# A layer norm ahead of the first matmuls, split over VectorE and ScalarE in a fixed order with dummy matmuls between

## The chip, the cores and the metric

The kernel runs on one core of a Trainium2 chip. The time is device time in microseconds (us) of one execution. Every set of runs was measured beside runs of the kernel before on the same chip, in alternating rounds. The core has one TensorE (PE, matmuls), one VectorE (DVE), one ScalarE (ACT), and a SyncE (SP) that issues most of the DMA transfers.

## The reference, cut to what matters

```python
x = A_x                                                # 2048 tokens x 1024
x = x + attention(layernorm(x), wqkv, wo)              # 32 heads of 32; each token sees 8 keys, 2 apart
x = x + swiglu(layernorm(x), w1, w3, w2)               # 1024 -> 3584 -> 1024
x = x + attention(layernorm(x), wqkv, wo)              # the same two layers again
x = x + swiglu(layernorm(x), w1, w3, w2)
```

The attention needs no large matmul for its scores. It is products and sums on VectorE. Projections and MLP are dense bf16 matmuls on TensorE. The first layer norm stands alone in front of everything: until its first chunk (512 tokens, four tiles of 128) is normalised and transposed, no real matmul can start. I call this stretch the prefix.

## The kernel before

TensorE's order is fixed by hand (`manual_schedule`). The order on VectorE, ScalarE and SyncE is decided by a scheduler, which works with priorities and with its own estimate of when things are ready.

```python
    x_sb = const.tile([P, S // P, D], BF16, name="x_sb")
    for j in range(TPC):                                   # TPC = 4 tiles in a chunk
        nc.sync.dma_start(x_sb[:, j:j + 1, :], xin[:, j:j + 1, :])
    ...
    for i in range(NWARM):                                 # 16 dummy matmuls, for the clock
        pw = bank("pw")
        nc.tensor.matmul(pw[:], lhsT=hT[:, 0, 0:P], rhs=hT[:, 0, :], start=True, stop=True)
    ...
        def stats(j):                                      # in ln_first, the prefix
            for hh in range(2):
                nc.vector.bn_stats(st[:, hh, :], x_sb[:, j, hh * 512:(hh + 1) * 512])
            nc.vector.bn_aggr(mv[:], st[:])
            nc.scalar.activation(sd[:], mv[:, 1:2], ACTF.Sqrt, bias=epst[:])
        def apply(j, mv, sd):
            nc.vector.reciprocal(rstd[:], sd[:])
            nc.vector.tensor_scalar(xn[:], x_sb[:, j, :], mv[:, 0:1], rstd[:], op0=ALU.subtract, op1=ALU.mult)
            for kk in range(KT):
                nc.tensor.transpose(pT[:, kk, :], xn[:, kk * P:(kk + 1) * P], ident[:])
            nc.scalar.copy(xnT[:, :, j * P:(j + 1) * P], pT[:])
    ...
    # q_part: "ps" matmuls of q, k or v of one chunk, copied out of PSUM by ScalarE, stored to DRAM
                nc.scalar.copy(sgt[:, t - t0, :], ps[:])   # sgt has 3 buffers
            nc.sync.dma_start(qkv_d[l][which][:, t0:t0 + SG, c * CH:(c + 1) * CH], sgt[:])
    # t_scores: loads qT and kT back, then on VectorE per window step w_
            nc.vector.tensor_tensor(pr[:], qT[:], kT[:, :, k0:k0 + TCH], op=ALU.mult)
            tree_sum8(pr, psm[:, w_, :])
    ...     # then transpose, sums, maximum, and on ScalarE
        nc.scalar.activation(E[:], L[:], ACTF.Exp, scale=scale)
    # b_stage: MLP; VectorE makes one hT tile per pair of matmul groups
                        nc.scalar.activation(sg[:], pg[:], ACTF.Silu)
                        nc.vector.tensor_tensor(hT[:, g0 + fi - f0, :], sg[:], pu[:], op=ALU.mult)
    # loads through SyncE's queue in program order: x chunks, wo (2 MB), w1t and w3t (1 MB each), kT, vT ...
```

## Time and profile before

The time before was 1636.41 us in the median of 3 runs (1635.89 to 1637.51). The span of the profiled run is 1635.4 us.

| what | value | view |
|---|---|---|
| TensorE / VectorE / ScalarE busy | 99% / 70% / 21% | page, part 1 |
| first real matmul (ps) | 13.92 us | timeline |
| first attention product (pr) | 56.59 us | timeline of VectorE |
| VectorE full | from 57 to about 530 us | slices of the page |
| TensorE's waits after the prefix | 0.66 + 4.86 + 2.11 + 1.86 + 0.75 = 10.2 us, the last at 425 us | timeline of TensorE |

From the page of the kernel before, the span, parts 1 and 2 (the digits are tenths of busy time in 40 slices of 41 us):

```profile
span 1635.4 us, 18944 instructions
...
PE 1616.1 (99%) x7472; PEld 800.2 (49%) x7472; DVE 1152.4 (70%) x1961; ACT 340.5 (21%) x530; POOL 1.9 (0%) x12
...
DVE  4899999999999781897728977299652992332212
```

TensorE is 99% busy, so a shorter prefix can give at most the time that TensorE loses there. VectorE is the second limit: it is full in slices 3 to 13. While it is full, TensorE waits for it now and then.

The timeline of the kernel before in the prefix (columns: start us, busy us, engine, line, operation, out<-in, form, count, and in brackets the idle time before it with its releaser):

```profile
3.81 1.29 DVE L149 BATCH_NORM_STATS2 st_165<-x_sb 128x6 f32<-128x512 bf16 x2 [2.53 <-DMA x_sb<-in_A_x_dram]
...
11.60 0.55 DVE L159 TENSOR_SCALAR xn<-x_sb,mv_215,rstd_235 128x1024 bf16<-128x1024 bf16 x1
12.20 0.62 PE L162 MATMUL pT<-ident,xn 128*128 128x128 bf16 x8 [0.96 <-DVE xn L159]
12.86 1.01 ACT L163 COPY xnT<-pT 128x1024 bf16<-128x1024 bf16 x1 [0.57 <-PE pT L162]
13.92 2.29 PE L202 MATMUL ps<-xnT,wqkv 128*128 128x512 bf16 x5 [1.10 <-ACT xnT L163]
```

The last tile is the bottleneck of the prefix: normalise, transpose, copy of 1.01 us, first matmul. The five matmuls in that last line take 2.29 us, 0.46 each, about twice what they take later (the whole stretch of 640 takes 139.71 us, 0.22 each). The clock shows why. The same kernel in stretches (from:to and length, then busy time and count by engine, granted TensorE clock, DMA share, GB/s):

```profile
13.50:17.00 3.50, 3.08 (x8) 1.27 (x8) 1.84 (x4) 0.37 (x1) 0.00 (x0) 0.53 1.05 387
195.00:210.00 15.00, 10.14 (x40) 4.24 (x39) 14.05 (x23) 7.66 (x12) 0.00 (x0) 0.89 0.89 254
```

The granted clock was 0.53 behind the first ps matmul: nearly the whole stretch at half speed. The clock record of the trace gives half speed from 13.40 to 16.81 us on the time axis of these views, 3.41 us (the prediction below means the same window, read 0.09 us late). Near 200 us, behind TensorE's longest wait, there is one more such window.

VectorE's timeline of the kernel before, at the start of attention:

```profile
56.59 2.36 DVE L228 TENSOR_TENSOR pr<-qT,kT 128x2048 bf16<-128x2048 bf16 x2 [3.38 <-DMA kT<-qkv_d_1_159]
...
86.08 0.43 DVE L247 TENSOR_TENSOR e_537<-E 128x256 f32<-128x256 bf16 x1 [0.70 <-ACT E L245]
```

The first product waited 3.38 us for kT. The issues on SyncE's queue of the kernel before, just ahead of that:

```profile
45.27 0.37 SPq L205 DMA_DIRECT2D qkv_d_1_159<-sgt  x1
45.69 0.46 SPq L356 DMA_DIRECT2D wo<-in_A_wo_dram  x1
48.87 0.53 SPq L213 DMA_DIRECT2D kT<-qkv_d_1_159  x1
...
53.91 0.47 SPq L297 DMA_DIRECT2D w1t<-in_B_w_dram  x1
```

kT can be issued when the last K store (45.27) has landed. Here wo goes behind that store and w1t behind kT.

TensorE's timeline of the kernel before, its waits after the prefix (between them it runs without a gap that matters):

```profile
187.09 8.85 PE L202 MATMUL ps<-xnT,wqkv 128*128 128x512 bf16 x40 [0.66 <-DVE x_sb L287]
200.80 3.28 PE L305 MATMUL pg<-xnT,w1t 128*128 128x512 bf16 x8 [4.86 <-DMA xnT<-xn]
263.25 24.56 PE L327 MATMUL acc<-w2t,hT 128*128 128x512 bf16 x113 [2.11 <-DVE hT L314]
347.30 18.52 PE L327 MATMUL acc<-w2t,hT 128*128 128x512 bf16 x85 [1.86 <-DVE hT L314]
425.06 24.56 PE L327 MATMUL acc<-w2t,hT 128*128 128x512 bf16 x113 [0.75 <-DVE hT L314]
```

At 507 us TensorE needs the 56th hT tile, the last of the second MLP unit (28 tiles each). In this profile that tile is finished at 507.26 us, just when it is needed, so no wait shows.

### The profile page before, as it was taken

How to read it: one execution, taken by the hardware profiler on the slowest of the kernel's cores; microseconds unless marked ns; L12 is line 12 of the kernel's file. 1: busy time of each engine (PE TensorE's matmuls, PEld its weight loads, DVE VectorE, ACT ScalarE, POOL GpSimd, SP SyncE). 2: the span in 40 equal slices, each digit the busy share in tenths (PEclk: the TensorE clock that was granted, in tenths of full speed). 3: DMA queues.
4: the chain of work that ended last, by engine and by line, in shares of the span. 5: the costliest groups of instructions: out<-in, count | busy, mean ns of one | idle time of the engine just before them, and what ended most of it. 6: DMA issues, size and time to landing. Idle time of an engine off the chain costs nothing.

```text
span 1635.4 us, 18944 instructions
## 1 busy us (share of the span) xinstructions
PE 1616.1 (99%) x7472; PEld 800.2 (49%) x7472; DVE 1152.4 (70%) x1961; ACT 340.5 (21%) x530; POOL 1.9 (0%) x12
## 2 busy tenths in 40 slices
PE   8999899999999999999999999999999999999999
PEld 5666444444444644446444554445544444444444
DVE  4899999999999781897728977299652992332212
ACT  3333311203021320223202232022320211121110
POOL 0000000000000000000000000000000000000000
PEclk9999999999999999999999999999999999999999
DMA  9943746557546774367743686438753574256440
GB/s 297 280 132 102 220 158 195 159 151 209 183 131 180 240 235 150 106 193 245 221 142 104 199 259 200 142 104 249 255 178 119 129 232 155 90 143 205 155 129 26
DMA packets 337113, 286.32 MB, mean 175 GB/s; under 512 B 69632, under 2 KB 319488, under 8 KB 336896
## 3 DMA queue, kind: packets, MB, share of 16 engines
q1 hardware_dynamic: 337024, 285.11, 57.2%
q8 instruction: 58, 0.95, 0.2%
q14 instruction: 31, 0.25, 0.0%
HBM read 239.99 MB, written 29.36 MB: 165 GB/s over the span
## 4 chain that ended last, share of the span: by engine, by line
PE 67%; DVE 29%; issue 3%; DMA 1%; ACT 0%; DVEq 0%; ACTq 0%
PE acc L327 21%; PE pg L305 15%; PE pu L309 15%; PE ps L202 13%; DVE pr L228 5%; DVE tm L273 4%; PE po L283 3%; DVE hT L314 3%; DVE tm L174 3%; DVE pr L174 2%; DVE x_sb L287 1%; DVE st L124 1%; DVE tm L175 1%; DVE pr L175 1%; DVE L L235 1%
## 5 line engine op out<-in xcount | busy, mean ns | idle before, releaser
L305 PE MATMUL pg<-xnT,w1t 128*128 128x512 bf16 x1792 | 424.7, 380 | 4.9 <-DMA xnT<-xn 4.9
L309 PE MATMUL pu<-xnT,w3t 128*128 128x512 bf16 x1792 | 423.7, 379 | 0.0
L327 PE MATMUL acc<-w2t,hT 128*128 128x512 bf16 x1792 | 390.8, 379 | 5.1 <-DVE hT L314 4.7
L202 PE MATMUL ps<-xnT,wqkv 128*128 128x512 bf16 x1536 | 334.3, 380 | 1.8 <-ACT xnT L163 1.1
L313 ACT ACTIVATE sg<-pg 128x512 bf16<-128x512 f32 x224 | 133.4, 597 | 843.2 <-PE pg L305 831.4
L314 DVE TENSOR_TENSOR hT<-sg,pu 128x512 bf16<-128x512 bf16 x224 | 152.1, 679 | 212.2 <-PE pu L309 210.7
L305 PEld LDWEIGHTS <-w1t 128*128 128x128 bf16 x1792 | 175.5, 98 | 217.0 <-issue 6.6
L327 PEld LDWEIGHTS <-hT 128*128 128x128 bf16 x1792 | 174.8, 98 | 218.5 <-DVE hT L314 9.0
L309 PEld LDWEIGHTS <-w3t 128*128 128x128 bf16 x1792 | 175.5, 98 | 212.0 <-issue 1.0
L202 PEld LDWEIGHTS <-wqkv 128*128 128x128 bf16 x1536 | 220.5, 144 | 114.6 <-issue 3.9
L332 DVE TENSOR_TENSOR x_sb<-x_sb,acc 128x512 bf16<-128x512 bf16 x128 | 87.0, 680 | 162.2 <-PE acc L327 162.2
L228 DVE TENSOR_TENSOR pr<-qT,kT 128x2048 bf16<-128x2048 bf16 x128 | 153.1, 1210 | 51.6 <-issue 32.1
L273 DVE TENSOR_TENSOR tm<-At,vT 128x2048 bf16<-128x2048 bf16 x128 | 151.7, 1213 | 0.3
L204 ACT CAST sgt<-ps 128x512 bf16<-128x512 f32 x192 | 108.7, 588 | 184.6 <-PE ps L202 151.7
L283 PE MATMUL po<-wo,oT 128*128 128x512 bf16 x512 | 115.4, 379 | 0.0
L124 DVE BATCH_NORM_STATS2 st<-x_sb 128x6 f32<-128x512 bf16 x120 | 79.9, 681 | 18.0 <-DMA x_sb<-in_A_x_dram 17.3
L174 DVE TENSOR_TENSOR pr<-pr 128x1024 bf16<-128x1024 bf16 x128 | 85.6, 680 | 0.0
L174 DVE TENSOR_TENSOR tm<-tm 128x1024 bf16<-128x1024 bf16 x128 | 84.4, 681 | 0.0
L283 PEld LDWEIGHTS <-oT 128*128 128x128 bf16 x512 | 50.0, 98 | 60.4
L287 DVE TENSOR_TENSOR x_sb<-x_sb,po 128x512 bf16<-128x512 bf16 x64 | 43.2, 677 | 15.4 <-PE po L283 15.4
L175 DVE TENSOR_TENSOR pr<-pr 128x512 bf16<-128x512 bf16 x128 | 51.8, 415 | 0.2
L175 DVE TENSOR_TENSOR tm<-tm 128x512 bf16<-128x512 bf16 x128 | 50.3, 415 | 0.1
(169 smaller groups left out, 428.7 us busy)
## 6 DMA issues: line engine op xcount, KB each, us to landing
w1t<-in_B_w_dram SPq DMA_DIRECT2D x56, 1024.0 KB, 5.4
w3t<-in_B_w_dram SPq DMA_DIRECT2D x56, 1024.0 KB, 7.2
w2t<-in_B_w_dram SPq DMA_DIRECT2D x48, 1024.0 KB, 5.4
wqkv<-in_A_wqkv_dram SPq DMA_DIRECT2D x28, 1024.0 KB, 6.6
w2t<-in_B_w_dram SPq DMA_DIRECT2D x16, 512.0 KB, 5.1
qkv_d_0_158<-sgt SPq DMA_DIRECT2D x16, 256.0 KB, 5.3
qkv_d_1_159<-sgt SPq DMA_DIRECT2D x16, 256.0 KB, 4.4
qT<-qkv_d_0_158 SPq DMA_DIRECT2D x8, 512.0 KB, 4.0
```

The costliest lines, as they stand in the source:

```text
L174: nc.vector.tensor_tensor(buf[:, 0:4, :], buf[:, 0:4, :], buf[:, 4:8, :], op=ALU.add)
L175: nc.vector.tensor_tensor(buf[:, 0:2, :], buf[:, 0:2, :], buf[:, 2:4, :], op=ALU.add)
L202: nc.tensor.matmul(ps[:], lhsT=ws[kk // KH][:, kk % KH, t::KT], rhs=xnT[:, kk, :], start=(kk == 0), stop=(kk == KT - 1))
L204: nc.scalar.copy(sgt[:, t - t0, :], ps[:])
L228: nc.vector.tensor_tensor(pr[:], qT[:], kT[:, :, k0:k0 + TCH], op=ALU.mult)
L273: nc.vector.tensor_tensor(tm[:], At[:], win, op=ALU.mult)
L283: nc.tensor.matmul(ps[:], lhsT=oT[:, t, j * P:(j + 1) * P], rhs=wo[:, t, hh * 512:(hh + 1) * 512], start=(t == 0), stop=(t == KT - 1))
L305: nc.tensor.matmul(pg[:], lhsT=w1t[:, kk, fi * P:(fi + 1) * P], rhs=xnT[:, kk, :], start=(kk == 0), stop=(kk == KT - 1))
L309: nc.tensor.matmul(pu[:], lhsT=w3t[:, kk, fi * P:(fi + 1) * P], rhs=xnT[:, kk, :], start=(kk == 0), stop=(kk == KT - 1))
L313: nc.scalar.activation(sg[:], pg[:], ACTF.Silu)
L314: nc.vector.tensor_tensor(hT[:, g0 + fi - f0, :], sg[:], pu[:], op=ALU.mult)
L327: nc.tensor.matmul(acc[:], lhsT=hT[:, f - f0, j * P:(j + 1) * P], rhs=w2ts[(f - f0) // 8][:, (f - f0) % 8, :], start=(f == f0), stop=(f == ...
```

## The change

The intent: make the prefix shorter and keep TensorE's clock up. The last tile's statistics go to ScalarE (a sum in one pass, a sum of squared deviations in a second). The order on VectorE and ScalarE is fixed by hand. The PSUM copies of the last two tiles are made in halves, one by each engine. Ten of the dummy matmuls stand between the transposes; 13 instead of 16 stand in front. Two of the four first loads are issued from ScalarE's queue.

```diff
-    NWARM = 16
+    NWARM = 13
 ...
-        nc.sync.dma_start(x_sb[:, j:j + 1, :], xin[:, j:j + 1, :])
+        (nc.scalar if j % 2 else nc.sync).dma_start(x_sb[:, j:j + 1, :], xin[:, j:j + 1, :])
 ...
+        def apply(j):
 ... (cut: as before; the last tile uses ScalarE's sums, (x + (-mean)) * rstd)
+            kn = KT if j < 2 else KT // 2
 ... (cut: transposes into KT // kn PSUM tiles)
+        def evacuate(j, pTs):
+            kn = KT // len(pTs)
+            for h, pT in enumerate(pTs):
+                copy = nc.vector.tensor_copy if h else nc.scalar.copy
+                copy(xnT[:, h * kn:(h + 1) * kn, j * P:(j + 1) * P], pT[:])
+
+        warm(NWARM)
+        with hp(), tc.manual_schedule(engines={mybir.EngineType.PE, mybir.EngineType.DVE,
+                                               mybir.EngineType.Activation}):
+            stats(0, 0)
+            stats(0, 1)
+            deviation(0)
+            stats(1, 0)
+            nc.scalar.activation(junk[:], x_sb[:, last, :], ACTF.Copy, accum_out=am[:, 0:1])
+            nc.scalar.mul(am[:, 1:2], am[:, 0:1], -1.0 / D)
+            pT0 = apply(0)
+            warm(4)
+            stats(1, 1)
+            deviation(1)
+            nc.scalar.activation(junk[:], x_sb[:, last, :], ACTF.Square, bias=am[:, 1:2], accum_out=am[:, 2:3])
+            stats(2, 0)
+            pT1 = apply(1)
+            warm(4)
+            evacuate(0, pT0)
+            deviation(last)
+            stats(2, 1)
+            deviation(2)
+            evacuate(1, pT1)
+            pT2 = apply(2)
+            warm(2)
+            pT3 = apply(3)
+            evacuate(2, pT2)
+            evacuate(3, pT3)
```

The diff ends in the prefix, but its effect does not. With different emission the scheduler also puts what follows in another order on VectorE, ScalarE and SyncE. In SyncE's queue wo moves ahead of the last K store, and w1t ahead of kT. On VectorE, hT and x_sb updates of the first two MLP units come 1 to 4 us of work earlier. In the traces VectorE has the same instructions ahead of the 56th hT tile in both orders, but for one short reciprocal, in another sequence; the sequences of VectorE and ScalarE become the same at about 531 us.

More of the change, by code (lines that the diff above doesn't have):

```diff
@@ L101, with warm @@
     nc.scalar.activation(preload[:], epst[:], ACTF.Sqrt)
-    for i in range(NWARM):
-        pw = bank("pw")
-        nc.tensor.matmul(pw[:], lhsT=hT[:, 0, 0:P], rhs=hT[:, 0, :], start=True, stop=True)
+    def warm(n):
+        for i in range(n):
+            pw = bank("pw")
+            nc.tensor.matmul(pw[:], lhsT=hT[:, 0, 0:P], rhs=hT[:, 0, :], start=True, stop=True)
     wo = const.tile([P, KT, D], BF16, name="wo")
@@ L143, in ln_first @@
         xnT = xnTs[key] = xtp.tile([P, KT, CH], BF16, name="xnT")
-        def stats(j):
-            st = small.tile([P, 2, 6], FP32, name="st1")
-            mv = small.tile([P, 2], FP32, name="mv1", bufs=2)
-            for hh in range(2):
-                nc.vector.bn_stats(st[:, hh, :], x_sb[:, j, hh * 512:(hh + 1) * 512])
-            nc.vector.bn_aggr(mv[:], st[:])
-            sd = small.tile([P, 1], FP32, name="sd1", bufs=2)
-            nc.scalar.activation(sd[:], mv[:, 1:2], ACTF.Sqrt, bias=epst[:])
-            return mv, sd
@@ L155, in apply @@
-        def apply(j, mv, sd):
-            rstd = small.tile([P, 1], FP32, name="rstd1")
-            nc.vector.reciprocal(rstd[:], sd[:])
-            xn = xnp.tile([P, D], BF16, name="xn")
-            nc.vector.tensor_scalar(xn[:], x_sb[:, j, :], mv[:, 0:1], rstd[:], op0=ALU.subtract, op1=ALU.mult)
-            pT = psum.tile([P, KT, P], BF16, name="pT", tag="mm")
-            for kk in range(KT):
-                nc.tensor.transpose(pT[:, kk, :], xn[:, kk * P:(kk + 1) * P], ident[:])
-            nc.scalar.copy(xnT[:, :, j * P:(j + 1) * P], pT[:])
@@ L165, in ln_first @@
-        with hp():
-            held = stats(0)
-            for j in range(1, TPC):
-                nxt = stats(j)
-                apply(j - 1, *held)
-                held = nxt
-            apply(TPC - 1, *held)
+        last = TPC - 1
+        st = small.tile([P, last, 2, 6], FP32, name="st1", bufs=1)
+        mv = small.tile([P, last, 2], FP32, name="mv1", bufs=1)
+        sd = small.tile([P, TPC], FP32, name="sd1", bufs=1)
+        rstd = small.tile([P, TPC], FP32, name="rstd1", bufs=1)
@@ new lines, in ln_first, with stats, deviation @@
+        am = small.tile([P, 3], FP32, name="am", bufs=1)
+        junk = xnp.tile([P, D], BF16, name="xn")
+        def stats(j, hh):
+            nc.vector.bn_stats(st[:, j, hh, :], x_sb[:, j, hh * 512:(hh + 1) * 512])
+        def deviation(j):
+            if j < last:
+                nc.vector.bn_aggr(mv[:, j, :], st[:, j, :, :])
+                nc.scalar.activation(sd[:, j:j + 1], mv[:, j, 1:2], ACTF.Sqrt, bias=epst[:])
+            else:
+                nc.scalar.activation(sd[:, j:j + 1], am[:, 2:3], ACTF.Sqrt, bias=epst[:], scale=1.0 / D)
@@ new lines, in apply @@
+        def apply(j):
+            nc.vector.reciprocal(rstd[:, j:j + 1], sd[:, j:j + 1])
+            xn = xnp.tile([P, D], BF16, name="xn")
+            if j < last:
+                nc.vector.tensor_scalar(xn[:], x_sb[:, j, :], mv[:, j, 0:1], rstd[:, j:j + 1],
+                                        op0=ALU.subtract, op1=ALU.mult)
+            else:
+                nc.vector.tensor_scalar(xn[:], x_sb[:, j, :], am[:, 1:2], rstd[:, j:j + 1],
+                                        op0=ALU.add, op1=ALU.mult)
+            kn = KT if j < 2 else KT // 2
+            pTs = []
+            for k0 in range(0, KT, kn):
+                pT = psum.tile([P, kn, P], BF16, name="pT", tag="mm")
+                for kk in range(k0, k0 + kn):
+                    nc.tensor.transpose(pT[:, kk - k0, :], xn[:, kk * P:(kk + 1) * P], ident[:])
+                pTs.append(pT)
+            return pTs
```

## The prediction

> **What bounds the kernel now.** The page: TensorE 99% busy, VectorE 70%. The timeline: real matmuls start at 13.92 us and run dense until 187 us. TensorE's waits up to 425 us are 0.66 (for x_sb), 4.86 (xnT at 200.8), 2.11, 1.86, 0.75 us (hT): 10.2 us., then none. The chain of waits runs through VectorE and DMA from 57 to 260 us, and the slices show VectorE full from 57 to about 530 us. So between 57 and 507 us the attention work on VectorE sets the pace, and TensorE has slack before it.
>
> **What the change does to the prefix.** Now: statistics from 3.81, last normalisation 11.60, last transposes 12.20, last PSUM copy 12.86 to 13.88 (1.01 us on ScalarE). The clock record shows TensorE at half speed from 13.49 to 16.90 (3.41 us): some 7 matmuls at 0.425 instead of 0.216 us, 1.5 us lost. The Trainium skill (TensorE: Matmul & The Clock Gate, Part 1) describes such an activity window of about 3.4 us; this trace agrees. The added 10 dummies should keep the clock up.
> Removed from VectorE: two statistics (2 x 0.6) and one aggregation. Added: two half copies out of PSUM, estimated 0.4 to 0.6 us each. ScalarE gets two passes over 1024 elements, estimated 1.0 us each from its 1.01 us copy, plus one small operation. Its work from 5.3 us on sums to 6.7 us and gaps. I expect ScalarE to be the prefix's limit and the first real matmul at 12.5 to 13.5 us. Issuing two loads from ScalarE saves only issue time (0.4 us each).
> TensorE should then be 2 to 2.5 us ahead at 20 us.
>
> **Why little of it should reach the end.** Attention starts at 56.59 us, when kT lands. The stores before it wait for ScalarE, which waits (2.2 us at 44.3) for statistics of x tiles whose load lands at 39.1; the DMA engines are nearly full from 28 to 60 us. This timing follows DMA, not TensorE. The instruction order also changes: wo's 2 MB load now precedes the last K store, and w1t's 1 MB load precedes kT. At 350 to 390 GB/s (estimate) kT lands 0 to 3 us later. In return the new VectorE order puts hT and x_sb updates of the first two MLP stages 1 to 4 us of work earlier, so the waits at 263 to 425 us shrink; but hT number 56 (507 us, which now finishes just in time) has the same VectorE work before it in both orders. So the end moves by what attention's start moves, about -2 to +3 us.
>
> **Prediction.** 1636.5 us, range 1632.8 to 1639.8. Faster by over 2%: 0.5%; within 2%: 99%; slower by over 2%: 0.5%.
>
> **What would show it.** Right: the first ps matmul near 13 us at full clock; the first pr later than 55.5 us; larger TensorE waits at 187/200 or 507 us, smaller ones at 263 and 347 us. Wrong on the prefix: half clock still behind the first ps matmul, or a start later than 13.9. Wrong on the absorption: pr starts 2 us earlier and the whole time falls by over 3 us.
>
> **What would make it wrong.** kT not delayed by the loads ahead of it; the reordered VectorE work shifting hT number 56; accumulating ScalarE passes costing much more than a copy; the clock window's phase, which decides also whether half clock returns after the wait at 200 us (about 1.7 us).

## The result, and the profile after

The changed kernel took 1637.5 us in the median of 6 runs (1635.92 to 1638.35), the kernel before 1636.84 us in the same rounds (6 runs, 1635.89 to 1637.71). Ratios here and below are those for the runs of the same rounds. They lie within 0.0002 of the ratio of the mean times, and are not quite the ratio of the quoted medians. The ratio is 1.0003 with a 95% interval of 0.999 to 1.0016: the same. The profiled run happens to be the fastest of the six. A second profile of the same kernel (e5 below, span 1636.3 us) has the same three waits, 5.52, 2.49 and 2.92 us.

From the page after, the span and part 1:

```profile
span 1633.9 us, 18952 instructions
...
PE 1616.6 (99%) x7479; PEld 800.8 (49%) x7479; DVE 1151.9 (70%) x1960; ACT 341.9 (21%) x534; POOL 1.9 (0%) x12
```

The timeline of the prefix after:

```profile
4.92 1.29 DVE L157 BATCH_NORM_STATS2 st_133<-x_sb 128x6 f32<-128x512 bf16 x2 [3.64 <-DMA x_sb<-in_A_x_dram]
...
6.69 1.04 ACT L197 ACTIVATE xn<-x_sb 128x1024 bf16<-128x1024 bf16 x1
...
7.63 0.19 ACT L197 ACTIVATION_READ_ACCUMULATOR xn<-x_sb 128x1 f32 x1
...
8.73 1.13 ACT L203 ACTIVATE xn<-x_sb,am 128x1024 bf16<-128x1024 bf16 x1
...
12.19 0.55 DVE L173 TENSOR_SCALAR xn<-x_sb,am,rstd_136 128x1024 bf16<-128x1024 bf16 x1
...
13.38 0.59 ACT L188 COPY xnT<-pT 128x512 bf16<-128x512 bf16 x1 [0.29 <-PE pT L180]
13.60 0.42 DVE L188 COPY xnT<-pT 128x512 bf16<-128x512 bf16 x1 [0.45 <-PE pT L180]
14.02 2.32 PE L247 MATMUL ps<-xnT,wqkv 128*128 128x512 bf16 x10 [0.45 <-ACT xnT L188]
```

The work itself became shorter: from the first statistics to the first ps matmul it is 14.02 - 4.92 = 9.10 us, before 13.92 - 3.81 = 10.11 us. But it starts 1.11 us later, because the first tile lands later, so the first matmul is not earlier. What did change is the pace: ten matmuls in 2.32 us, not five in 2.29 us. The half copies, 0.59 us on ScalarE and 0.42 us on VectorE, replace the one of 1.01 us. The stretches after:

```profile
13.50:17.00 3.50, 3.05 (x16) 2.01 (x14) 3.15 (x7) 1.05 (x2) 0.00 (x0) 1.00 1.05 390
195.00:210.00 15.00, 11.31 (x40) 4.59 (x41) 14.03 (x21) 5.55 (x10) 0.00 (x0) 0.77 0.80 228
```

The clock stays full behind the first matmul (1.00 for 0.53). Near 200 us it is worse in this run, two windows at half speed for one. The first copy of a finished ps tile starts at 15.94 us for 17.26 us before, so TensorE is 1.3 us ahead there.

VectorE's timeline after, at the start of attention:

```profile
57.29 2.36 DVE L273 TENSOR_TENSOR pr<-qT,kT 128x2048 bf16<-128x2048 bf16 x2 [7.82 <-DMA kT<-qkv_d_1_127]
```

The issues on SyncE's queue after, ahead of that:

```profile
40.22 0.91 SPq L401 DMA_DIRECT2D wo<-in_A_wo_dram  x1
43.15 0.36 SPq L250 DMA_DIRECT2D qkv_d_1_127<-sgt  x1
...
46.32 0.46 SPq L342 DMA_DIRECT2D w1t<-in_B_w_dram  x1
52.19 0.52 SPq L258 DMA_DIRECT2D kT<-qkv_d_1_127  x1
```

The last K store is issued 2.1 us earlier than before, and VectorE is ready far earlier (it waits 7.82 us, not 3.38). But kT is issued 9.0 us after that store instead of 3.6 us, now that wo is in the queue ahead of the store and w1t ahead of kT. So attention starts 0.7 us later than before, not earlier.

TensorE's waits after the prefix:

```profile
198.69 3.57 PE L350 MATMUL pg<-xnT,w1t 128*128 128x512 bf16 x8 [4.94 <-DMA xnT<-xn]
343.72 18.52 PE L372 MATMUL acc<-w2t,hT 128*128 128x512 bf16 x85 [1.59 <-DVE hT L359]
505.85 18.52 PE L372 MATMUL acc<-w2t,hT 128*128 128x512 bf16 x85 [2.91 <-DVE hT L359]
```

The waits at 187, 263 and 425 us are gone. Those of 2.11 and 0.75 us (2.86 together) were for hT, and a new wait for hT of 2.91 us has come at 506 us, at the 56th tile. TensorE arrives there earlier and waits for VectorE instead. The sum is 9.4 us, before 10.2 us.

### The profile page after: what moved, and what is told of

Read it like the earlier page. It is cut to its first block, busy times and chain, and to the rows that moved or that the text cites. A ratio compares the mean times of both kernels' runs of the same rounds, so it can differ in the third digit from the quotient of the medians.

```text
span 1633.9 us, 18952 instructions
## 1 busy us (share of the span) xinstructions
PE 1616.6 (99%) x7479; PEld 800.8 (49%) x7479; DVE 1151.9 (70%) x1960; ACT 341.9 (21%) x534; POOL 1.9 (0%) x12
## 4 chain that ended last, share of the span: by engine, by line
PE 68%; DVE 27%; issue 2%; DMA 2%; ACT 1%; SPq 0%; DVEq 0%
PE acc L372 21%; PE pg L350 17%; PE pu L354 16%; PE ps L247 10%; DVE pr L273 5%; DVE tm L318 4%; PE po L328 3%; DVE hT L359 2%; DVE tm L219 2%; DVE pr L219 2%; DVE st L127 2%; DVE x_sb L332 1%; DVE pr L220 1%; DVE tm L220 1%; DVE oT L221 1%
```

## The experiments

Two theories stood against each other at the start.

- A, "absorbed": what the prefix gains is lost on the way, because attention's start and its VectorE work set the end. What the changed order of later instructions does is a second, separate effect.
- B, "nothing gained": the prefix itself gains nothing (the first matmul is no earlier), the dummies are idle ornament, and the order does not matter.

To separate prefix and order I pinned the order of everything after the prefix on SyncE, VectorE and ScalarE, by a list, with dependencies that order instructions without any semaphore. Pinning the changed kernel to its own order gave the identical instruction order on every engine. All experiments but e5 carry this addition:

```diff
+PINNED = {"SP": [...], "DVE": [...], "ACT": [...]}     # emission numbers, in the wanted order
 ...
+    names = {i.name: i for i in nc.cur_bb.bb.instructions}
+    for todo in PINNED.values():
+        for first, then in zip(todo, todo[1:]):
+            tc.add_manual_dep(names[f"I-{BASE[0] + then}"], f"I-{BASE[0] + first}",
+                              mybir.DependencyInfo(mybir.DependencyClass.NoSync, mybir.DependencyReason.DATA),
+                              reason="pinned order")
```

All runs at a glance. "First E" is the start of VectorE's first sum after the exponential (e<-E). "Wait at 507" is TensorE's wait for the 56th hT tile, with the time at which it ends. The profile columns are each from one run; e1 and e12 are the same kernel, and so are "after" and e5, so their differences show how far two runs can lie apart.

| run | median us, it / before | ratio, 95% interval | first pr us | first E us | wait at 507: us, end |
|---|---|---|---|---|---|
| before | as in the rows below | | 56.59 | 86.08 | none |
| after | 1637.5 / 1636.84 | 1.0003, 0.999 to 1.0016 | 57.29 | 85.28 | 2.91, 505.85 |
| e1 new prefix, old order | 1635.77 / 1637.56 | 0.9988, 0.9974 to 1.0001 | 56.22 | 85.50 | none |
| e2 old prefix, new order | 1640.77 / 1637.56 | 1.0018, 1.0006 to 1.0031 | 59.48 | 88.16 | 2.92, 508.80 |
| e3 less VectorE work early | 1633.62 / 1637.56 | 0.9977, 0.9965 to 0.999 | 57.72 | 82.22 | 2.91, 502.84 |
| e4 less VectorE work late | 1638.48 / 1637.56 | 1.0003, 0.999 to 1.0017 | 57.65 | 85.65 | 2.92, 506.27 |
| e5 changed kernel again | 1638.42 / 1637.68 | 1.0004, 0.9992 to 1.0017 | 57.91 | 85.91 | 2.92, 506.54 |
| e6 one queue | 1638.47 / 1637.68 | 1.0006, 0.9993 to 1.0018 | 57.59 | 86.17 | 2.91, 506.79 |
| e7 no dummies between | 1639.79 / 1637.68 | 1.0013, 0.9999 to 1.0026 | 60.12 | 88.17 | 2.91, 508.80 |
| e8 kT first | 1638.79 / 1637.68 | 1.001, 0.9998 to 1.0023 | 51.20 | 87.86 | 2.91, 508.48 |
| e9 loads late | 1636.55 / 1637.03 | 0.9993, 0.9981 to 1.0006 | 51.80 | 84.38 | 2.91, 504.94 |
| e10 attempt at a best | 1644.69 / 1637.03 | 1.0046, 1.0034 to 1.0059 | 50.68 | 93.06 | 2.90, 513.64 |
| e11 e10 with old prefix | 1647.65 / 1637.03 | 1.0063, 1.0051 to 1.0076 | 53.97 | 96.19 | 2.91, 516.91 |
| e12 e1 again | 1635.58 / 1637.03 | 0.9992, 0.9978 to 1.0005 | 55.36 | 84.26 | none |

e1 to e4, e5 to e8 and e9 to e12 shared a chip each, three different chips. None reaches 2%; what counts below are intervals and positions in the traces. e3 and e4 give wrong results on purpose; all others are correct.

### e1 and e2: prefix and order, crossed

e1 is the changed prefix with the order that the kernel before has after it. e2 is the old prefix with the changed kernel's order. The edit is the pinned list:

```diff
-PINNED = {"SP": [... qT, wo, last K store, V store, w1t, kT, ...], ...}        # changed kernel's
+PINNED = {"SP": [... qT, last K store, wo, kT, V stores, w1t, ...], ...}       # e1: as before
```

> The changed prefix, but every engine's instructions after the prefix held in the order of the kernel before. Theory A (the end follows the start of attention on VectorE, and the scheduler's new order of loads, wo and w1t ahead of kT, gave the gain back): the x loads of the third chunk land near 37 us as in the changed kernel, kT lands and the first pr starts at 54 to 55.5 us (57.29 in the changed kernel, 56.59 before), and the total is 1 to 2.5 us below before and 1.5 to 3 us below the changed kernel. Rival B (the prefix itself gains nothing, the order is of no weight): first pr near 56.6 and total within 0.7 us of before. Rival C (half clock after the wait at 200 us takes the gain): first pr earlier, but half clock for 6.8 us or more near 200 us and no gain.

> The prefix of before, with every engine's later instructions in the order of the changed kernel. Theory A: the first pr starts at 58.5 to 60 us, TensorE waits 3 us or more for hT number 56 near 505 us, and the total is 1.5 to 3 us above before. Rival B: total within 0.7 us of before.

e1 took 1635.77 us, e2 1640.77 us, the kernel before 1637.56 us. The new prefix with the old order is about 0.12% faster than before (the interval just touches 1), the new order with the old prefix is 0.18% slower (the interval excludes 1). The sum of the two, +0.06%, is near what both together gave (+0.03% and +0.04%). So the change is two effects that cancel: the prefix is worth 1.3 to 2 us (0.08% in e12, 0.12% here), and the order it brings with it costs 2 to 3 us (0.12% from e12 to e5, 0.18% here). Of theory B only "the first matmul is no earlier" holds. Theory A falls in part too: in the old order what the prefix gains is not absorbed, it reaches the end (e12 below). e1's first pr, 56.22 us, came later than the 54 to 55.5 us that I had expected; its profile is of the slowest of its five runs.

### e3 and e4: does VectorE's attention work set the end?

e3 replaces the wide product and its sums by eight columns for three of the eight window steps of the very first score stage, which takes 5.22 us of work off VectorE at 70 to 78 us. e4 does the same in a later stage (second layer, third chunk), where VectorE has slack by the slices.

```diff
+            if l == 0 and tcx == 0 and w_ >= 5:        # e4: l == 1 and tcx == 4
+                few = pr[:, 0, 0:8]
+                nc.vector.tensor_tensor(few, qT[:, 0, 0:8], kT[:, 0, k0:k0 + 8], op=ALU.mult)
+                nc.vector.tensor_tensor(few, few, few, op=ALU.add)
+                nc.vector.tensor_tensor(few, few, few, op=ALU.add)
+                nc.vector.tensor_tensor(psm[:, w_, :], qT[:, 0, :], kT[:, 0, k0:k0 + TCH], op=ALU.mult)
+                continue
```

> The changed kernel in its own order, with 3 of 8 windows of the very first score stage cut to a few elements: some 5.4 us less VectorE work near 65 us (result wrong on purpose for the first 256 tokens). Theory A (VectorE work between 57 and 507 us sets the end): total 4 to 5.5 us below the changed kernel, and the waits of TensorE near 200 and 505 us shrink by about as much in sum. Rival D (TensorE alone is the limit, its waits are chance): within 1 us.

> The same cut of three windows, but in layer 2 (after 560 us), where VectorE has idle time. Theory A: total within 1 us of the changed kernel. Rival (any VectorE work counts): 4 to 5.5 us less.

VectorE's timeline in e3, where the first sum after the exponential starts:

```profile
82.22 0.42 DVE L307 TENSOR_TENSOR e<-E 128x256 f32<-128x256 bf16 x1 [2.49 <-ACT E L305]
```

TensorE's timeline in e3, its wait for the 56th hT tile:

```profile
502.84 20.21 PE L387 MATMUL acc<-w2t,hT 128*128 128x512 bf16 x85 [2.91 <-DVE hT L374]
```

VectorE's timeline in e4 at the same sum:

```profile
85.65 0.43 DVE L307 TENSOR_TENSOR e<-E 128x256 f32<-128x256 bf16 x1 [0.70 <-ACT E L305]
```

TensorE's timeline in e4 at the same wait:

```profile
506.27 18.52 PE L387 MATMUL acc<-w2t,hT 128*128 128x512 bf16 x85 [2.92 <-DVE hT L374]
```

Of the 5.22 us, 1.79 us are given back at once: the exponential on ScalarE is now what VectorE waits for (2.49 us for 0.70 us). The other 3.43 us (85.65 - 82.22) appear 420 us later to the hundredth: 506.27 - 502.84 = 3.43. The mean time of e3 is 1633.9 us, of e4 1638.1 us. e4 alone changed nothing against the changed kernel. So from the first sum after the exponential to about 506 us the chain on VectorE sets the pace, one to one, and later it does not.

The table says the same for every run. The 56th tile's instruction starts 419.84 to 420.01 us after the first E in all eleven profiles with the new order, and 420.50 to 420.54 us after it in the three with the old order (before, e1, e12). From the first pr to the first E, however, it takes between 24.5 us (e3) and 42.4 us (e10). So it is the first E, not the first pr, from which the end can be told.

There is a second thing in these two lines: the 85 matmuls behind the wait took 20.21 us in e3 and 18.52 us in e4. The clock was 0.93 over 500 to 525 us in e3 and 1.00 in e4. That is one window at half speed, 1.69 us, behind the 2.9 us wait. It falls in some executions and not in others. Taking the end of that wait from the span leaves 1128.1 us in the four profiles without that window (after, e4, e8, e9) and 1129.8 us in the six with one (e2, e3, e5, e6, e7, e11). e10 has two (21.44 us for the 85 matmuls), which begin 0.9 us before the wait ends, and 1131.1 us. The kernel before has no wait there, and the 56th hT tile's 507.26 us leaves 1128.1 us; e1 and e12, whose tiles end at 506.72 and 505.45 us, leave 1128.2 us. So the end of a run is: when VectorE's chain has made that tile, plus 1128.1 us, plus 1.7 us if the clock fell. This explains why the profile of the changed kernel (1633.9) looks better than its median: it is the run without this window, while e5's has it.

### e5: the changed kernel again

The file is unchanged and serves as the partner of e6 to e8 on one chip.

> The changed kernel again, so that it shares its rounds with the next three. Both theories: within 1 us of its first median (1637.5), first pr between 56.8 and 58 us.

1638.42 us, ratio 1.0004. The waits are 5.52, 2.49 and 2.92 us. The result repeats.

### e6: all four first loads on one queue

```diff
-        (nc.scalar if j % 2 else nc.sync).dma_start(x_sb[:, j:j + 1, :], xin[:, j:j + 1, :])
+        nc.sync.dma_start(x_sb[:, j:j + 1, :], xin[:, j:j + 1, :])
```

> The changed kernel in its own later order, but with all four x loads issued from SyncE again. The first statistics then start about 1.1 us earlier (near 3.8 us) and the first real matmul at 12.8 to 13.4 us instead of 14.02; but the weight loads and the load of the second chunk's x queue up 0.9 us later, so that x lands near 15.1 instead of 14.3 us. Theory A (the start of attention counts, and it follows the loads): first pr 0.3 to 1 us later than in the changed kernel, total 0 to 1.5 us above it. Rival B (the end follows the first real matmul): total about 1 us below it.

The first statistics start at 3.53 us and the first ps matmul at 13.24 us, 0.8 us earlier than in e5 (14.06). So it was the split over two queues that delayed the first tile. Yet the first pr came at 57.59 us (e5 57.91), the wait at 507 us ended at 506.79 us (506.54), and the time is the same, so rival B of the expectation falls. The earlier first matmul bought nothing here, and ScalarE's timeline shows where most of it goes. Its square roots of the second chunk's norm start at 19.75 us (e5 19.92). In e5 they stand behind the copies of the first ps tiles; in e6 the copies are done earlier, and the square roots wait 0.54 us for VectorE's statistics of the second chunk's x, which start at 14.62 us (e5 14.42) when that x has landed. So 0.17 of the 0.8 us come through, and kT is issued only 0.3 us earlier (52.58 us, e5 52.88).

### e7: the dummies between the transposes taken out

```diff
-    NWARM = 13
+    NWARM = 16
 ...
-            warm(4)        # and the other warm(4) and the warm(2)
```

> The changed kernel in its own later order, with the 10 dummy matmuls between the transposes taken out (16 in front again). The first real matmul stays near 14 us; half clock for one window or two (3.4 or 6.8 us) falls on the last transposes and the first real matmuls, TensorE is 1.5 us or more late at 20 us. Theory A: first pr unchanged within 0.5 us, total within 0.7 us of the changed kernel, the loss being taken out of TensorE's wait near 200 us. Rival B: total 1.5 us or more above it.

This missed my expectation. The first ps matmul was at the same place (14.06 us), but everything after it came later. The stretch behind the first matmul in e7 (columns as above):

```profile
13.50:17.00 3.50, 3.25 (x10) 1.32 (x9) 3.15 (x7) 0.51 (x1) 0.00 (x0) 0.50 1.05 391
```

Half speed: by the clock record the clock fell at 11.10 us for 6.83 us. ScalarE's timeline in e5, the first copy of a ps tile and the square roots of the second chunk's norm:

```profile
15.99 0.59 ACT L249 CAST sgt<-ps 128x512 bf16<-128x512 f32 x1 [1.98 <-PE ps L247]
...
19.92 0.48 ACT L131 ACTIVATE sd<-mv,epst 128x2 f32<-128x2 f32 x2
```

The same two on ScalarE in e7:

```profile
17.67 0.59 ACT L254 CAST sgt<-ps 128x512 bf16<-128x512 f32 x1 [3.66 <-PE ps L252]
...
21.81 0.48 ACT L138 ACTIVATE sd<-mv,epst 128x2 f32<-128x2 f32 x2
```

The square roots (sd) of the second chunk's norm stand in ScalarE's fixed order behind the copies of the first three ps tiles. Slower ps matmuls therefore delay the square roots (1.89 us), which delay that norm's transposes. These, and the first stores of ps tiles, stand in SyncE's queue ahead of the load of the third chunk's x. So that chunk's statistics start at 39.19 us for 37.51 us in e5, and the first pr at 60.12 us for 57.91 us. The wait at 507 us ends at 508.80 us for 506.54 us, and the median is 1639.79 us for 1638.42 us. The intervals of the two ratios overlap, so the time alone does not prove it, but the trace follows the 2 us through every step. So TensorE's pace right after the prefix does reach attention's start, by the in-order queues of ScalarE and SyncE.

And this is where the prefix's gain in e1 comes from: the kept clock, not an earlier first matmul. e2, the old prefix in the same order, bears this out: its first copy of a ps tile starts at 17.65 us (e7 17.67), its wait at 507 us ends at 508.80 us as in e7, and its span is 1638.6 us as in e7. Without the dummies the new prefix gains nothing over the old one there. Both profiles have two half-speed windows at this place (e2 from 11.48 to 18.31 us) where the kernel before has one, so what the prefix is worth also depends on how these windows fall.

### e8: kT ahead of wo and w1t

```diff
-PINNED = {"SP": [... qT, wo, last K store, V store, w1t, kT, V store, V store, w3t, ...]}
+PINNED = {"SP": [... qT, last K store, V store, kT, wo, w1t, V store, V store, w3t, ...]}
```

> The changed kernel in its own later order but for two loads on SyncE: wo and w1t are issued right after kT instead of ahead of it. Theory A: kT lands 5 us or more earlier, the first pr starts at 49.5 to 52 us; part of it is lost again to a VectorE wait for the transposes of the third chunk (60 to 62 us), so that hT number 56 and the total come 1.5 to 4 us earlier than in the changed kernel. Rival B: total unchanged within 0.7 us.

The first half of the expectation held and the second did not. The first pr came at 51.20 us, 6.7 us earlier than in e5. So the two loads ahead of it are what delays kT in the changed kernel. But VectorE then waits again; its timeline in e8:

```profile
65.77 0.55 DVE L143 TENSOR_SCALAR xn<-x_sb,mv,rstd 128x1024 bf16<-128x1024 bf16 x1 [7.65 <-DMA xnT<-xn]
...
87.86 0.42 DVE L300 TENSOR_TENSOR e<-E 128x256 f32<-128x256 bf16 x1 [0.70 <-ACT E L298]
```

The next normalisation waits 7.65 us for the DMA transposes of the ones before it. The wait was moved, not removed, and more than the gain is lost: the first E comes at 87.86 us (e5 85.91), and the wait at 507 us ends at 508.48 us, 1.94 us later than in e5, where I had expected it 1.5 to 4 us earlier. An earlier attention start is thus not yet an earlier end.

### e9: wo, w1t and w3t behind the whole first attention load

```diff
-PINNED = {"SP": [... qT, last K store, V store, kT, wo, w1t, V stores, w3t, 3 transposes, ...]}
+PINNED = {"SP": [... qT, last K store, V store, kT, V stores, 3 transposes, V store, Q store, transpose, Q store, vT, wo, w1t, w3t, ...]}
```

> The changed kernel in its own later order but for SyncE: the loads of wo, w1t and w3t (4 MB, first needed near 150 and 200 us) go behind kT, the third chunk's transposes and vT. Theory A': attention is held by what queues in front of both kT and those transposes. First pr at 49.5 to 51.5 us, VectorE's wait for the transposes 4 us or less (7.65 us in the run before with only wo and w1t moved), hT number 56 and the total 3 to 5.5 us earlier than in the changed kernel. Rival: another limit holds the total within 1 us.

The waits for transposes shrank to 0.77 and 0.59 us, so those three loads were what held the transposes up. The first pr was at 51.80 us. Yet the time fell by only about 0.1% against the changed kernel (ratio 0.9993 for e5's 1.0004), less than I had expected. VectorE's first use of the exponential came at 84.38 us (e5 85.91). ScalarE's timeline in e9 ahead of it:

```profile
80.35 2.05 ACT L257 CAST sgt<-ps 128x512 bf16<-128x512 f32 x4 [7.08 <-DMA qkv_d<-sgt]
82.42 1.28 ACT L298 ACT_TABLE_LOAD   x1
83.72 0.63 ACT L298 ACTIVATE E<-L 128x512 bf16<-128x512 f32 x1
```

The exponential stands behind four PSUM copies in ScalarE's order. Those wait 7.08 us for a store to free one of three buffers. Then the table for the exponential is loaded, 1.28 us. In the kernel before, that table is loaded at 80.06 us, long before E's input is ready at 85.4 us, and costs nothing. So the 6 us gained at the start of attention came down to 1.5 us at the exponential, and the wait at 507 us ended 1.6 us earlier than in e5.

### e10 and e11: an attempt at a best, and the same with the old prefix

Beside e9's queue, e10 moves the last K tile's copy ahead of two square roots on ScalarE, and moves what is left of the norms of the third and fourth chunk out of the first score loop to the place behind it.

```diff
-PINNED = {"DVE": [... last xn of chunk 3, statistics of chunk 4 amid the pr loop, ...], "ACT": [... sd, sd, K copy, ...]}
+PINNED = {"DVE": [... pr loop, last xn of chunk 3, statistics of chunk 4, psmT, ...], "ACT": [... K copy, sd, sd, ...]}
```

> As the last, and also: the copy that fills the last K store goes ahead of two square roots on ScalarE, and the normalisations of the third and fourth chunk stand behind all eight score windows on VectorE, so that VectorE doesn't wait for the transposes. Theory A': first pr at 48.5 to 50.5 us and no VectorE wait over 1 us up to 75 us; TensorE's waits near 200 and 505 us shrink to 2 us or less each; total 5 to 9 us below the changed kernel (1629.5 to 1633.5), below both kernels.

> The same later order as the last with the prefix of the kernel before. If the half-clock stretch of the old prefix counts once nothing else holds TensorE or attention, the total is 1 to 2.5 us above the last; if it is absorbed, within 0.5 us.

e10 was a clear miss: 1644.69 us, ratio 1.0046, slower than everything so far. VectorE's timeline in e10, at the same sum as in e3 and e4:

```profile
93.06 0.42 DVE L300 TENSOR_TENSOR e<-E 128x256 f32<-128x256 bf16 x1 [15.29 <-ACT E L298]
```

ScalarE's timeline in e10 ahead of that:

```profile
70.10 0.30 ACT L138 ACTIVATE sd<-mv,epst 128x2 f32<-128x2 f32 x1 [7.27 <-DVE mv L135]
...
89.03 2.05 ACT L257 CAST sgt<-ps 128x512 bf16<-128x512 f32 x4 [14.49 <-DMA qkv_d<-sgt]
91.11 1.28 ACT L298 ACT_TABLE_LOAD   x1
92.40 0.63 ACT L298 ACTIVATE E<-L 128x512 bf16<-128x512 f32 x1
```

With the norm later on VectorE, ScalarE's square root waits 7.27 us, and the transposes that need it come later. SyncE's queue stands at the transpose until 69.45 us, and the stores stand behind it with the three large loads. So ScalarE's copies wait 14.49 us for store buffers, and the exponential waits with them; VectorE then waits 15.29 us. TensorE too waits once, 3.28 us at 89.67 us, for a copied PSUM tile. What I had taken for an interruption of the score loop was work that keeps three other queues going.

e11 took 1647.65 us. Its wait at 507 us ends at 516.91 us for 513.64 us in e10, so in this order the prefix is worth 3.3 us there, and 3.0 us by the medians, more than the 1 to 2.5 us expected; the intervals of the two ratios only just overlap. The prefix is worth something in all three orders tried. e11's profile again has two half-speed windows behind the prefix (12.31 to 19.13 us) where the kernel before has one, so the different worth need not come from the order.

### e12: e1 once more

The same kernel as e1, on another chip.

> The changed prefix with the later order of before, for a second profile and to share rounds with the last three: total again 1 to 2.5 us below before; first pr between 54 and 56.5 us.

1635.58 us for 1637.03 us, ratio 0.9992 (0.9978 to 1.0005). Twice, on two chips, it came out 0.08% to 0.12% below the kernel before. Each interval just reaches 1. Of all versions that give the right result it has the lowest ratio, though the gain is under 2 us. The profile of e12 has a span of 1633.6 us, with the half-speed window behind the first matmul gone and one left near 200 us as before (granted clock 1.00 over 13.5 to 17 us and 0.89 over 195 to 210 us). Its waits are those of the kernel before (0.47, 4.85, 2.15, 1.86 and 0.75 us), each 1.8 us earlier: at 198.97 for 200.80 us, and at 423.24 for 425.06 us. It has no wait and no half speed at 507 us.

## Why the prediction was right or wrong

The predicted 1636.5 us is 1.0 us from the measured 1637.5 us, and the range holds it. Part of the core of the argument was right: the chain on VectorE sets the end (e3 moves it one to one), and the end did not follow the first matmul (e6). But it moves with the first E and not with attention's start as such: in e8 the first pr came 6.7 us earlier and the end of the wait at 507 us 1.94 us later. Right in detail were the full clock behind the first ps matmul, the first pr later than 55.5 us (57.29), the wait at 263 us gone, and a larger wait at 507 us (2.91 us). Also right was that wo and w1t ahead of kT cost attention's start (e8: kT first brings it 6.7 us earlier).

These steps were wrong, and partly made up for one another. In the old order the prefix's gain of 1.3 to 2 us reaches the end (e1, e12), against the prediction's "little of it should reach the end", and the new order took 2 to 3 us back. So the closeness of the number is partly luck, and the range of 7 us was wide beside effects of 2 to 3 us.

- "the first real matmul at 12.5 to 13.5 us": it was 14.02 us, which is also later than the 13.9 us that the prediction named as the sign of being wrong on the prefix. The chain itself was shortened by 1.0 us as hoped; the mis-sized term is the start. I took the first tile's landing from before (3.81 us), and its statistics started at 4.92 us with the loads split over two queues. With one queue (e6) they started at 3.53 us and the first matmul came at 13.24 us, inside the predicted range. So the step "Issuing two loads from ScalarE saves only issue time" failed: it also delayed the first tile. That the tiles in flight side by side are the reason fits, but no run separates it from the weight loads, which are also issued earlier (1.68 us for 2.60 us).
- "TensorE should then be 2 to 2.5 us ahead at 20 us": it was 1.3 us ahead (first PSUM copy at 15.94 for 17.26 us). The kept clock, about 1.5 us, was sized well. The earlier first matmul, 0.4 to 1.4 us, did not come.
- "This timing follows DMA, not TensorE": e7 refutes it as it stands. Without the dummies TensorE was about 1.9 us slower after the prefix, and attention started 2.2 us later. The mechanism is that ScalarE's square roots and SyncE's loads stand in fixed order behind TensorE's results.
- "kT lands 0 to 3 us later" by the order: the new prefix starts pr 1.1 to 2.6 us later with the new order (57.29 and 57.91 in after and e5, 56.22 and 55.36 in e1 and e12), and the old prefix 2.9 us later (59.48 for 56.59). The size was right. The prediction set the gain of the prefix against nothing there, though: the new prefix brings pr forward by 0.4 to 1.2 us in the old order, and by 1.6 to 2.2 us in the new one.
- "smaller ones at 263 and 347 us": the wait at 347 us was 1.59 and 2.49 us in two profiles for 1.86 us before; not clearly smaller.
- "the clock window's phase" was named as a risk for the wait at 200 us. It also acts at 507 us: the new wait there brings one window at half speed in some executions, 1.7 us, which the old order never showed, as it has no wait there.

The account can be closed with the profiles. From e12 (new prefix, old order) to e5 (new prefix, new order) the span grows by 2.7 us (1633.6 to 1636.3): 1.0 us because the 56th tile is finished at 506.49 us for 505.45 us, and 1.7 us for the clock window. From before to e12 it shrinks by 1.8 us (to e1, the same kernel, by 0.5 us). Together it is +0.9 us, beside a difference of the medians of 0.7 us.

What stays open: how the order's cost splits between the queues. I changed SyncE's alone (e8, e9) but never VectorE's or ScalarE's alone in a way that worked. The positions bound it. Behind the first E VectorE's new order does not cost time, it is 0.6 us shorter up to the 56th tile (419.9 for 420.5 us). The cost lies ahead of the first E (88.16 us in e2 for 86.08 us before; with the new prefix 85.28 and 85.91 us for 85.50 and 84.26 us, where two runs of one kernel lie 0.6 and 1.2 us apart) and in the clock window behind the new wait, 1.7 us. Part of e2's lateness can be its second half-speed window behind the prefix. Where the rest of e6's 0.8 us goes behind kT is not shown.

## What to carry to other kernels

An edit in one place of a program that a scheduler orders changes the order everywhere after it, so compare the instruction order before costing the edit, and cross the two effects (new edit in the old order, old edit in the new order) before judging either. When an engine's chain sets the pace for hundreds of microseconds, only what moves that chain as a whole counts, and an earlier start can be lost again at its next wait (e8, e9, e10), so measure at a late point of the chain; follow it through the in-order queues, where one late copy or store holds up what stands behind it. A wait of 3 us on TensorE costs more than its length when the clock falls behind it, and whether it does differs from run to run.

## What the Trainium skill lacked or had wrong

- "TensorE: Matmul & The Clock Gate", Part 1: it says that the clock halves after at least one idle window of about 3.4 us, free-running. The windows agree (3.41 and 6.83 us). It lacks how much activity still counts as idle. In the 3.41 us ahead of the fall, TensorE was busy for 1.24 us (36%) in the kernel before and for 1.13 us (33%) in e7, with transposes only. The windows ahead of those, with 2.13 us (62%) and 2.16 us (63%), did not bring the clock down. So single bursts of transposes didn't keep it up here, and a few dummy matmuls between them did. The clock records of all fourteen profiles give more. Each profile is cut into windows of 3.413 us so that its first fall lies on a border (in the kernel before the falls at 13.40, 201.13 and 1634.73 us lie 55 and 475 windows apart). From full clock, all 28 windows with at most 1.40 us (41%) of busy TensorE were followed by half clock, and all with 1.70 us (50%) or more by full clock; of the 12 between, one was followed by half clock (1.64 us, e11). From half clock, all 14 with at most 2.53 us (74%) were followed by half clock again, and all 26 with 2.89 us (85%) or more by full clock.
- The same page, same part: it says that what half clock costs varies from run to run with the phase of the free-running window. This agrees, and here it has a price: the same wait of 2.9 us was followed by 85 matmuls in 18.52 us or in 20.21 us. In "after" the wait lies across two windows, and the emptier one still has 1.64 us of busy TensorE; in e5 the window ahead of the fall has 0.50 us.
- "DMA: Bandwidth & Descriptors", section "Issuing engines are not separate DMA queues": it says that issuing from several engines saves only issue time, and that transfers interleave. It lacks that the split can cost the first of several tiles time: that tile's statistics started at 4.92 us (after) and 4.78 us (e7) with two queues, and at 3.53 us (e6) and 3.81 us (before) with one. That interleaving is the reason is not shown.
- "ScalarE: Activation LUTs", section "What ACT_TABLE_LOAD costs": its formulas, 186 ns or 280 ns (bias as an operand) plus 0.833 ns per element, give estimates of 1.04 and 1.13 us for 1024 elements, and the trace has just these. It gives no time for the accumulator output: each pass is followed by an ACTIVATION_READ_ACCUMULATOR of 0.19 us, which starts 0.1 us before the pass ends.
- The same section gives 1283 ns for the table load plus some 1380 ns of drain for every switch. The trace has 1.28 us for the load. The drain does not show where it would delay the work: in e9 the copies end at 82.40 us and E starts at 83.72 us, 1.32 us later, and in e10 it is 1.32 us too.
